# One more pair of chunks transposed on TensorE, and one load issued earlier, in a fused retention and MLP kernel

## The chip, the cores and the metric

The kernel runs on one NeuronCore of a Trainium2 chip. The metric is the device time of one execution in microseconds (us), lower is better. Every comparison of times is made between executions on the same chip.

## The reference, cut to what matters

The operation is a retention layer (attention without softmax, with a decay mask) followed by a two-layer MLP with the Mish activation. All inputs and the output are fp32.

```python
# q, k, v: [8 batches, 8 heads, 576 positions, 64]
scores = scale * np.matmul(q, k.transpose(0, 1, 3, 2))          # scale = 1/8
gamma  = 1.0 - 2.0 ** (-5.0 - np.arange(H))                     # one decay per head
Dmat   = np.where(rel >= 0, gamma[:, None, None] ** rel, 0.0)   # rel = i - j, causal
attn   = np.matmul(scores * Dmat, v)
x      = attn.transpose(0, 2, 1, 3).reshape(8 * 576, 512)       # 4608 tokens
h      = x @ w_in                                               # 512 -> 2048
g      = h * np.tanh(np.log1p(np.exp(h)))                       # Mish
out    = g @ w_out                                              # 2048 -> 512
```

## The kernel before: the parts that matter here

The 4608 tokens are 36 chunks of 128 tokens. Two chunks, `2m` and `2m + 1`, make a **pair** `m` (0 to 17), and four chunks make a **tile of tokens** `t` (0 to 8), the unit of the MLP. The kernel is one hand-ordered program: matmuls of the MLP, which fill TensorE (PE), are interleaved with the smaller steps of the retention, which prepare the tokens that the MLP needs next. The order on each engine is the order of the code.

The life of a pair `m`, from load to x:

- `load(m)`: GpSimd (POOL) issues three DMAs, q, k and v of both chunks. They go into buffers that rotate (4 for q and k), so `load(m)` waits until `step_p(m - 4)` has read the old contents.
- `step_p(m)`: VectorE (DVE) multiplies q and k by the decay factors into `qks`, in bf16, tokens on partitions. Four instructions to a pair.
- `step_t(n)`: q and k have to be turned, so that the head dimension lies on partitions (`qkT`). There are two ways. For chunks below `NPE`, PE transposes eight 128x128 blocks to a chunk (against an identity matrix) into PSUM, and then ScalarE (ACT) copies q's half and DVE k's half into `qkT`. From `NPE` on, one DMA, issued by SyncE (SP), transposes all 16 blocks of the pair from SBUF to SBUF.
- `step_s(n)`: PE computes the scores, DVE applies the mask (`sm`).
- `pair_o(m)`: PE adds up the state (`step_k`), then the products within the chunk and across chunks; DVE casts the sum into `xT`, the MLP's input.

```python
    NPE = 14
    # ...
    def step_t(n):
        m, u = divmod(n, 2)
        r = pairs[m]
        if "qk" not in r:
            r["qk"] = tr.tile([P, 2, 2, NP, P], BF16, name="qkT", bufs=3)
        if n >= NPE:
            nc.sync.dma_start_transpose(out=r["qk"].rearrange("p i u n t -> p (i u n) t"),
                                          in_=r["qks"].rearrange("p i u h d -> p (i u h d)"))
            return
        tp = ps_sc.tile([P, 4, NP, P], BF16, name="sc")[:, ::2]
        for i in range(2):
            flat = r["qks"][:, i, u].rearrange("p h d -> p (h d)")
            for p in range(NP):
                nc.tensor.transpose(tp[:, i, p, :], flat[:, ts(p, P)], ident)
        for i, copy in enumerate((nc.scalar.copy, nc.vector.tensor_copy)):
            copy(r["qk"][:, i, u], tp[:, i])
```

The part of the schedule that the change touches. `g1(t, i)` is the i-th of 16 steps of the MLP's first product (four matmuls of 512 columns, then Mish on ACT), `g2(t, i)` a quarter of a 128-token output tile (four matmuls); `one(n, "T")` and `one(n, "S")` call `step_t(n)` and `step_s(n)`. `cross(m)` is the transposing DMA, and it has a tail: GpSimd copies one element of the result, so that nothing which GpSimd issues later, above all the next `load`, starts before the transpose has landed.

```python
    def visit(m, w):
        n = 2 * m
        if w == 0:
            if 2 * m + 2 < NPE:
                load(m + 4)
        elif w == 2:
            if m == 5:
                step_sum(*step_k(1))
            if n < NPE:
                one(n, "T")
        elif w == 3 and n < NPE:
            one(n + 1, "T")
        elif w == 5:
            one(n, "S")
            one(n + 1, "S")
        elif w == 6 and m == 6:
            step_p(7)
        elif w == 7 and m < 6:
            pair_o(m, lambda: step_p(m + 1))

    def cross(m):
        step_t(2 * m)
        nc.gpsimd.tensor_copy(seen, pairs[m]["qk"][0:1, 0, 0, 0, 0:1])
    # ...
    for i in range(nF):                     # nF = 16
        visit(6 + i // 8, i % 8)            # pairs 6 and 7
        if i == 8:
            cross(7)
            load(10)
            step_p(8)
        elif i == 10:
            cross(8)
            load(11)
        g1(2, i)
        if i % 8 == 7:
            pair_o(6 + i // 8)
            if i == 15:
                scores(8)                   # step_s(16), step_s(17)
            for j in range(4):
                g2(1, 8 + i // 2 - 3 + j)

    for t in range(3, nT + 1):              # the steady loop
        for i in range(nF):
            m, w = 2 * (t + 1) + i // 8, i % 8
            if m + 1 < n_pairs and w == 0:
                step_p(m + 1)
            elif m + 1 < n_pairs and w == 2:
                cross(m + 1)
                load(m + 4)
            if t < nT:
                g1(t, i)
            if i % 4 == 3:
                if m < n_pairs and w == 7:
                    pair_o(m)
                    if m + 1 < n_pairs:
                        scores(m + 1)
                for j in range(4):
                    if t < nT or i < 12:
                        g2(t - 1, i - 3 + j)
```

So with `NPE = 14` pairs 0 to 6 are turned by PE and pairs 7 to 17 by DMA, and `load(10)` and `load(11)` each stand behind a transposing DMA.

Of the kernel before, what the change touches and what calls it, by code (L numbers as in the profile page):

```python
# [17 lines left out]
def kernel(  # L18
# [30 lines left out]
    nF = d_ff // P  # L49
    KC = d_model // P  # L50
    NCH = 4
    NPE = 14


    chunks = []
# [41 lines left out]
    def load(m):  # L97
        if m >= n_pairs:
            return
        r = pairs[m] = {}  # L100
        r["q"] = io.tile([P, 2, H, D], F32, name="qraw")
        r["k"] = io.tile([P, 2, H, D], F32, name="kraw")
        if m < NCH // 2:
            r["v"] = io.tile([P, 2, H, D], F32, name="vraw", bufs=NCH // 2)
            return
        r["vs"] = tok.tile([P, 2, H, D], BF16, name="v", bufs=5)
        if m < NCH:
            return
        for x, src in (("q", q), ("k", k), ("vs", v)):
            off = 0  # L110
            for b, i0, ni in chunks[2 * m]:
                nc.gpsimd.dma_start(  # L112
                    out=r[x][ds(off, ni)].rearrange("p u h d -> p (u h) d"),
                    in_=src[ds(b, 2), :, ds(i0, ni), :].rearrange("b h p d -> p (b h) d"))
                off += ni
# [139 lines left out]
    def step_p(m, us=(0, 1)):  # L255

        r = pairs[m]
        if "qks" not in r:
            r["qks"] = io.tile([P, 2, 2, H, D], BF16, name="qks")
            r["ks"] = r["qks"][:, 1]  # L260
        for u in us:
            for i, (x, g) in enumerate((("q", gq), ("k", gk))):
                nc.vector.tensor_tensor(  # L263
                    by_slots(r["qks"][:, i, u]), r[x][:, u].rearrange("p (r s) d -> p r s d", r=2),
                    g[:, place(2 * m), :].rearrange("p (r s) -> p r s", r=2).unsqueeze(3).to_broadcast([P, 2, NP, D]),
                    op=OP.mult)
# [18 lines that stand above are left out]
# [39 lines left out]
    def step_k(m):  # L324

        if m >= n_pairs or len(chunks[2 * m]) > 1:
            return None
        b, i0, _ = chunks[2 * m][0]
        ks, vs = pairs[m]["ks"], pairs[m]["vs"]

        if m < 6:
            st = ps_sc.tile([P, 2, 2, NP, 64], F32, name="sc")[:, 0]
        else:
            st = ps_h.tile([P, 2, NP, 64], F32, name="hp")
        for u in range(2):
            for p in range(NP):
                for e in range(2):
                    nc.tensor.matmul(st[ds(64 * e, 64), u, p, :], lhsT=ks[:, u, 2 * p + e, :],  # L338
                                     rhs=vs[:, u, 4 * e + p, :],
                                     start=(u == 0 and p == 0), stop=True, skip_group_check=True)  # L340
        return b, i0, st

    def step_sum(b, i0, st):

        if i0 == 0:
            st_sum[b] = tr.tile([P, 2, NP, 64], F32, name="st")
            nc.vector.tensor_copy(st_sum[b], st)
        else:
            nc.vector.tensor_tensor(st_sum[b], st_sum[b], st, op=OP.add)  # L349
        ssb = tr.tile([P, 2, NP, 64], BF16, name="ssb", bufs=6)  # L350
        (nc.vector.tensor_copy if b < 4 and i0 < 2 * P else nc.scalar.copy)(ssb, st_sum[b])  # L351
        for u in range(2):
            st_sb[b + u, i0 + P] = ssb[:, u]
# [41 lines left out]
    def pair_o(m, then=None):  # L395

        sc = pairs[m][1][0]
        ot = sc.rearrange("p e (g u) i -> p e g u i", g=2)
        state = step_k(m)
        for u in range(2):  # L400
            within(pairs[m]["vs"][:, u], pairs[m][u][1], ot[:, :, :, u, :], u == 0)
        for u in range(2):
            across(2 * m + u, ot[:, :, :, u, :])
        xt, s = x_of(2 * m)
        xv = xt[:, :, ds(s * P, 2 * P)].rearrange("p (e g) (u i) -> p e g u i", e=2, u=2)
        if m == 5:

            nc.scalar.copy(xv[:, 0], ot[:, 0])
            nc.vector.tensor_copy(xv[:, 1], ot[:, 1])
        else:  # L410
            nc.vector.tensor_copy(xv.rearrange("p e g u i -> p (e g) u i"), ot.rearrange("p e g u i -> p (e g) u i"))  # L411
        if then:
            then()
        if state:
            step_sum(*state)
# [5 lines left out]
    def g1(t, f):  # L421
        if f == 0:
            gts[t] = gp.tile([P, nF, NCH * P], BF16, name="gT")
        hp = ps_h.tile([P, NCH * P], F32, name="hp")
        for c in range(KC):
            nc.tensor.matmul(hp, lhsT=w_in_t[:, c, ts(f, P)], rhs=xts[t][:, c, :],  # L426
                             start=(c == 0), stop=(c == KC - 1))
        nc.scalar.activation(gts[t][:, f, :], hp, AX.Mish)  # L428
# [24 lines left out]
    def g2(t, i):  # L453
        s, part = divmod(i, 4)
        if t == nT - 1:
            s = (s + 2) % 4
        if part == 0:
            outs[t] = ps_h.tile([P, d_model], F32, name="hp")
        ops = outs[t]
        for f in range(4 * part, 4 * part + 4):  # L460
            nc.tensor.matmul(ops, lhsT=gts[t][:, f, ts(s, P)], rhs=w_out_t[:, f, :],  # L461
                             start=(f == 0), stop=(f == nF - 1))
        if part == 3:
            store(t, s, ops, nc.scalar.copy)
# [24 lines left out]
    def one(n, steps):  # L489
        for step in steps:  # L490
            if step == "P":
                step_p(n // 2, (n % 2,))
            else:
                {"T": step_t, "S": step_s, "O": step_o}[step](n)
# [96 lines left out]
# [6 lines that stand above are left out]
        elif w == 2:  # L597
            if m == 5:
                step_sum(*step_k(1))
            if n < NPE:  # L600
                one(n, "T")
        elif w == 3 and n < NPE:
            one(n + 1, "T")
        elif w == 5:
            one(n, "S")
# [11 lines that stand above are left out]
    def scores(m):  # L617
        one(2 * m, "S")
        one(2 * m + 1, "S")
# [3 lines left out]
    for i in range(nF):  # L623
        if i == 4:
            step_p(4)
        elif i >= 8:
            visit(4, i % 8)
        g2(0, i)
    for i in range(8):
        visit(5, i)  # L630
        g2(1, i)
    for i in range(nF):
        visit(6 + i // 8, i % 8)
        if i == 8:
            cross(7)
            load(10)
            step_p(8)
        elif i == 10:
            cross(8)
# [5 lines that stand above are left out]
                scores(8)  # L645
            for j in range(4):
                g2(1, 8 + i // 2 - 3 + j)

    for t in range(3, nT + 1):
        for i in range(nF):  # L650
            m, w = 2 * (t + 1) + i // 8, i % 8
# [46 lines left out]
```

## Time and profile before

| | |
|---|---|
| device time, three executions | 316.04, 316.23 and 316.77 us, median 316.23 |
| span of the profiled execution (316.77 us) | 315.0 us |
| PE busy | 299.9 us, 95% of the span |
| ACT, DVE, POOL busy | 134.8, 121.3, 79.2 us |
| DMA | 43.90 MB, mean 139 GB/s |
| transposing DMAs of `qks` into `qkT` | 11, issue to landing 4.2 us at least, 4.3 median, 10.4 at most |

How to read the profile's lines: times are us from the start of the span unless marked ns. PE is the matmul stream and PEld the weight loads beside it; SPq is the queue of SyncE, which issues DMAs. `L282` is line 282 of the kernel: L282 is the transpose on PE, L284 its copies to SBUF, L275 the transposing DMA, L112 the loads, L615 the one-element copy of `cross`, L308 the scores, L426 the MLP's first product, L461 its second, L484 the output's stores. `out<-in` names the tiles, and what stands in square brackets is the engine's idle time before the instruction and what ended it. The chain of waits is the sequence of work that ended last, followed backwards from the end.

### The profile page before, as it was taken

The numbers are of one execution on the slowest core, as the hardware profiler recorded it, in microseconds if no ns is written. First come the engines' busy times: TensorE is split into PE (matmuls) and PEld (weight loads), VectorE is DVE, ScalarE is ACT, GpSimd is POOL, SyncE is SP. The second block draws the span as 40 slices with busy tenths as digits, with TensorE's granted clock in tenths as the row PEclk, the third lists the DMA queues.
The fourth block names the chain that finished last, engine by engine and source line by source line (L and its number), as shares of the span: only waits on it lengthen the run. The fifth ranks groups of instructions, "written<-read, shape, count | busy, mean of one in ns | idle before, by whom it ended". The sixth has DMA issues, their size and how long they took to land.

```text
span 315.0 us, 6021 instructions
## 1 busy us (share of the span) xinstructions
PE 299.9 (95%) x2585; PEld 157.0 (50%) x2621; DVE 121.3 (38%) x170; ACT 134.8 (43%) x236; POOL 79.2 (25%) x103
## 2 busy tenths in 40 slices
PE   7799999999999898999999999999999999999995
PEld 3355588655554444444445454545454544444444
DVE  3456474218687471608080807070717141000000
ACT  7565656420464343344444434343434343334311
POOL 6676772543300620422404040500000000000000
PEclk9799999999999999999999999999999999999999
DMA  5999999999982999699797969793132300000032
GB/s 150 264 182 229 199 207 223 203 227 255 205 140 54 190 204 178 144 167 197 161 146 152 152 126 178 155 160 85 53 82 56 80 33 35 33 33 33 35 83 83
DMA packets 74026, 43.90 MB, mean 139 GB/s; under 512 B 57744, under 2 KB 65168, under 8 KB 74000
## 3 DMA queue, kind: packets, MB, share of 16 engines
q0 software_dynamic: 43424, 26.22, 56.4%
q1 hardware_dynamic: 30432, 17.18, 22.1%
q8 instruction: 20, 0.33, 0.5%
q10 hardware_dynamic: 144, 0.13, 0.1%
q14 instruction: 6, 0.05, 0.0%
HBM read 36.70 MB, written 9.44 MB: 146 GB/s over the span
## 4 chain that ended last, share of the span: by engine, by line
PE 83%; DMA 6%; ACT 4%; issue 2%; DVE 2%; SPq 1%; ACTq 0%; DVEq 0%
PE hp L461 37%; PE hp L426 29%; DMA qkT<-qks 5%; PE hp L449 4%; PE sc L308 3%; PE sc L360 3%; ACT res L481 2%; PE sc L374 1%; SPq L142 1%; DMA kraw<-in_k_dram 1%; PE hp L338 1%; PE hp L473 1%; PE sc L282 1%; PE hp L437 1%; ACT qkT L284 1%
## 5 line engine op out<-in xcount | busy, mean ns | idle before, releaser
L461 PE MATMUL hp<-w_out_t,gT 128*128 128x512 bf16 x541 | 125.2, 379 | 1.2 <-issue 0.3
L426 PE MATMUL hp<-xT,w_in_t 128*128 128x512 bf16 x480 | 112.6, 379 | 1.0
L428 ACT ACTIVATE gT<-hp 128x512 bf16<-128x512 f32 x124 | 74.0, 597 | 37.8 <-PE hp L426 35.2
L461 PEld LDWEIGHTS <-gT 128*128 128x128 bf16 x560 | 53.3, 98 | 62.7
L426 PEld LDWEIGHTS <-w_in_t 128*128 128x128 bf16 x496 | 47.7, 97 | 57.1 <-issue 0.3
L481 ACT COPY res<-hp 128x512 f32<-128x512 f32 x35 | 20.5, 586 | 81.4 <-PE hp L461 81.4
L411 DVE CAST xT<-sc 128x1024 bf16<-128x1024 f32 x13 | 15.9, 1224 | 97.3 <-PE sc L374 78.3
L318 DVE TENSOR_TENSOR sm<-sc,mask 128x1024 bf16<-128x1024 f32 x34 | 40.3, 1219 | 11.5 <-PE sc L308 11.5
L615 POOL COPY seen<-qkT 1x1 bf16<-1x1 bf16 x11 | 1.9, 177 | 130.8 <-DMA qkT<-qks 130.8
L263 DVE TENSOR_TENSOR qks<-kraw,gk 128x512 bf16<-128x512 f32 x32 | 21.9, 685 | 1.7 <-DMA kraw<-in_k_dram 1.7
L351 ACT CAST ssb<-st 128x512 bf16<-128x512 f32 x12 | 7.4, 618 | 34.5 <-DVE st L349 30.4
L263 DVE TENSOR_TENSOR qks<-qraw,gq 128x512 bf16<-128x512 f32 x32 | 21.9, 684 | 0.7 <-DMA qraw<-in_q_dram 0.7
L112 POOL DMA_DIRECT2D qraw<-in_q_dram x16 | 17.4, 1087 | 8.7 <-issue 3.5
L112 POOL DMA_DIRECT2D kraw<-in_k_dram x16 | 17.2, 1076 | 8.6 <-issue 4.1
L112 POOL DMA_DIRECT2D v<-in_v_dram x16 | 17.3, 1081 | 7.2 <-DMA kraw<-in_k_dram 2.5
L476 DVE COPY half<-hp 128x256 f32<-128x256 f32 x1 | 0.4, 424 | 43.8 <-PE hp L473 43.8
L449 PE MATMUL hp<-xT,w_in_t 128*128 128x128 bf16 x272 | 16.9, 219 | 0.2 <-ACT gT L451 0.2
L308 PE MATMUL sc<-qkT 64*128 64x128 bf16 x288 | 12.2, 220 | 4.4 <-DMA qkT<-qks 3.0
L449 PEld LDWEIGHTS <-w_in_t 128*128 128x128 bf16 x272 | 15.5, 98 | 0.9 <-issue 0.4
L308 PEld LDWEIGHTS <-qkT 64*128 64x128 bf16 x288 | 8.2, 95 | 10.3 <-DMA qkT<-qks 3.6
L451 ACT ACTIVATE gT<-hp 128x512 bf16<-128x512 f32 x17 | 10.0, 596 | 6.7 <-PE hp L449 6.7
L360 PE MATMUL sc<-sm,v 128*64 128x128 bf16 x288 | 12.2, 223 | 0.5 <-DVE sm L314 0.2
(70 smaller groups left out, 154.2 us busy)
## 6 DMA issues: line engine op xcount, KB each, us to landing
out_dram<-res SPq DMA_DIRECT2D x31, 256.0 KB, 2.1
qraw<-in_q_dram POOLq DMA_DIRECT2D x12, 512.0 KB, 8.2
kraw<-in_k_dram POOLq DMA_DIRECT2D x12, 512.0 KB, 9.7
v<-in_v_dram POOLq DMA_DIRECT2D x12, 256.0 KB, 10.6
qraw<-in_q_dram POOLq DMA_DIRECT2D x8, 256.0 KB, 9.7
kraw<-in_k_dram POOLq DMA_DIRECT2D x8, 256.0 KB, 9.4
w_out_t<-in_moe_w_out_dram POOLq DMA_DIRECT2D x4, 512.0 KB, 11.4
qraw<-in_q_dram SPq DMA_DIRECT2D x8, 128.0 KB, 3.3
```

The source lines that it names most:

```text
L112: nc.gpsimd.dma_start(out=r[x][ds(off, ni)].rearrange("p u h d -> p (u h) d"), in_=src[ds(b, 2), :, ds(i0, ni), :].rearrange("b h p d -> p ...
L263: nc.vector.tensor_tensor(by_slots(r["qks"][:, i, u]), r[x][:, u].rearrange("p (r s) d -> p r s d", r=2), g[:, place(2 * m), :].rearrange( ...
L308: nc.tensor.matmul(sc[:, e, p, :], lhsT=qk[r, 1, u, p, :], rhs=qk[r, 0, u, p, :], start=True, stop=True)
L318: nc.vector.tensor_tensor(sm.rearrange("p e n i -> p (e n) i"), sc.rearrange("p e n i -> p (e n) i"), mask1.rearrange("p e n i -> p (e n) ...
L360: nc.tensor.matmul(ot[ds(64 * c, 64), e, g, :], lhsT=vs[:, h, :], rhs=sm[:, e, p, :], start=(start and g == 0), stop=True, skip_group_chec ...
L411: nc.vector.tensor_copy(xv.rearrange("p e g u i -> p (e g) u i"), ot.rearrange("p e g u i -> p (e g) u i"))
L426: nc.tensor.matmul(hp, lhsT=w_in_t[:, c, ts(f, P)], rhs=xts[t][:, c, :], start=(c == 0), stop=(c == KC - 1))
L428: nc.scalar.activation(gts[t][:, f, :], hp, AX.Mish)
L449: nc.tensor.matmul(hp[:, j, :], lhsT=w_in_t[:, c, ts(4 * fb + j, P)], rhs=xts[t][:, c, ts(s, P)], start=(c == 0), stop=(c == KC - 1))
L451: nc.scalar.activation(gts[t][:, ds(4 * fb, 4), ts(s, P)], hp, AX.Mish)
L461: nc.tensor.matmul(ops, lhsT=gts[t][:, f, ts(s, P)], rhs=w_out_t[:, f, :], start=(f == 0), stop=(f == nF - 1))
L481: copy(ot, ops)
```

## The change

`NPE` goes from 14 to 16, so that pair 7 (chunks 14 and 15) is turned by PE and ACT/DVE copies, as pairs 4 to 6 are, and no longer by a DMA. Its two `step_t` calls then fall in `visit(7, 2)` and `visit(7, 3)`, two and three steps of `g1` after the place where the DMA was called. With `cross(7)` its one-element copy on GpSimd goes. The load of pair 10 moves as well: `visit(6, 0)` now issues it (`2 * 6 + 2 < 16`), eight steps of `g1` earlier, with no transposing DMA ahead of it. `load(11)` stays behind `cross(8)`.

The purpose is to take away a wait of PE for the DMA transpose of pair 7 where PE has plenty of matmuls to place around it, and to spread the loads of pairs 10 and 11.

```diff
-    NPE = 14
+    NPE = 16
@@ visit
         elif w == 2:
             if m == 5:
                 step_sum(*step_k(1))
-            if n < NPE:
-                one(n, "T")
-        elif w == 3 and n < NPE:
+            one(n, "T")
+        elif w == 3:
             one(n + 1, "T")
@@ first products of tile 2, second half of tile 1's second product
     for i in range(nF):
         visit(6 + i // 8, i % 8)
         if i == 8:
-            cross(7)
-            load(10)
             step_p(8)
         elif i == 10:
             cross(8)
```

In the order of instructions PE gains 16 transposes of 128x128 (eight ahead of step 10 of `g1(2, ...)` and eight ahead of step 11), ACT and DVE two copies of 128x512 each; SP loses one transposing DMA and GpSimd one copy. Nothing else moves.

## The prediction

> **What bounds the kernel now.** I read the first two parts of the page, then the chain of waits, then PE's timeline and windows around the changed place, and last the queues that PE waits for there. The page first: PE's total, PE by slice of 7.9 us, and the DMA's share by slice.
>
> ```profile
> PE 299.9 (95%) x2585; PEld 157.0 (50%) x2621; DVE 121.3 (38%) x170; ACT 134.8 (43%) x236; POOL 79.2 (25%) x103
> ...
> PE   7799999999999898999999999999999999999995
> ...
> DMA  5999999999982999699797969793132300000032
> ```
>
> PE is the bound from start to end. After the first two slices, which are start-up and not touched, only the 14th and the 16th slice (102 to 110 us and 118 to 126 us) fall to 8. In the 12th and 13th slice (87 to 102 us) the DMA share drops to 8 and 2 tenths: the DMA engines have nothing to do just ahead of the first dip. The chain of waits names both dips; here each stands between the pieces around it (start, length, what).
>
> ```profile
> 88.92 0.45 PE sc L282 x8
> ...
> 99.07 1.13 PE hp L426 x6
> 100.20 4.59 DMA qkT<-qks
> 104.79 0.05 issue
> 104.83 0.62 PE sc L308 x16
> ...
> 113.43 2.50 PE hp L426 x12
> 115.93 10.40 DMA qkT<-qks
> 126.33 0.05 issue
> 126.38 0.62 PE sc L308 x16
> ```
>
> These are the only two places where the end hangs on a transposing DMA: pair 7's, issued at 100.20 and landed after 4.59 us, and pair 9's, issued at 115.93, which took 10.40 us. PE has other work during most of both. What it really loses is the bracket in its timeline, the idle time ahead of the scores:
>
> ```profile
> 104.83 0.62 PE L308 MATMUL sc<-qkT 64*128 64x128 bf16 x16 [1.43 <-DMA qkT<-qks]
> ...
> 126.38 0.62 PE L308 MATMUL sc<-qkT 64*128 64x128 bf16 x16 [1.61 <-DMA qkT<-qks]
> ```
>
> The same view with all other scores shows no such bracket after these two: from 132 us on the windows give PE 15.58 us busy in each 15.70. So 1.43 + 1.61 = 3.04 us are at stake, 1.0% of the span, and no more. Why the second DMA took 10.40 us stands in the timelines of SP and POOL:
>
> ```profile
> 77.87 1.16 POOL L112 DMA_DIRECT2D qraw<-in_q_dram  x1 [2.67 <-DVE qks L263]
> ...
> 104.84 0.18 POOL L615 COPY seen<-qkT 1x1 bf16<-1x1 bf16 x1 [23.06 <-DMA qkT<-qks]
> 105.52 1.15 POOL L112 DMA_DIRECT2D qraw<-in_q_dram  x1 [0.50 <-issue]
> ...
> 111.35 1.17 POOL L112 DMA_DIRECT2D v<-in_v_dram  x1
> ```
>
> POOL finishes issuing load 9 at 81.8, then stands 23.06 us behind pair 7's transpose, and then issues loads 10 and 11 together from 105.5 to 112.5. The transpose of pair 9 goes out into that backlog. In the list of windows, 96 to 100 us has a DMA share of 0.00, and 112 to 120 us one of 1.66 and 1.22.
>
> **What the Trainium skill says.** "VectorE: DVE Perf Modes", section "The three transpose paths", puts a 128x128 bf16 transpose at 390 ns on TensorE and 1309 ns by DMA. "TensorE: Matmul & The Clock Gate", section "Part 4: PE-mode transpose", adds about 275 ns in a kernel, and that PSUM has to be copied out. The trace has 219 ns for one, and eight in 0.45 us on the chain (56 ns each), since they are pipelined; the measured 0.45 is what I use. The DMA moves 16 blocks in 4.59 us, 287 ns each, far less than the page's single block. "DMA: Bandwidth & Descriptors", section "Issuing engines are not separate DMA queues", says that DMAs run on the same 16 engines and interleave, whoever issues them. The trace agrees: landing times of the transpose go from 4.2 us on idle engines to 10.40 beside the two loads. The same page, section "Queues, rings and completion order", has each engine take turns between queues by packets, so a transpose is slowed, not held until a load is done.
>
> **The change part by part.**
>
> *Removed: pair 7's DMA and the wait for it.* PE no longer waits for it at 103.41. That is -1.43 us.
>
> *Added on PE: 16 transposes* in two groups of eight, each between steps of `g1`. Two rows of the chain show a group between such steps, at 87.61 and 88.92 us, 0.45 us each, with PE going on at once. So +0.90 us. The scores' own 0.55 us and everything else stay.
>
> *Are these scores ready in time?* PE reaches step 10 of this stretch at 98.91 plus two steps of 0.865 (20 matmuls in 4.33 us), with the chain's boundary some 0.15 later: about 100.8. The first group ends near 101.2, the second near 102.6. The input is there, since DVE multiplied pair 7 by 96.2. ACT needs 0.58 us to a copy and DVE 0.42, one after the other: the second group is in SBUF at about 103.2 to 103.8, with room for a Mish of 0.60 ahead of it. The scores start at about 103.41 + 0.90 = 104.3. So no wait, with 0.5 us in hand, just what pair 6 has (its copy ends at 90.48, its scores start at 91.02). On ACT there are 0.60 + 0.58 = 1.18 us of work to a step of 0.865 + 0.45 = 1.31, so the Mish steps keep up; the two PSUM banks of `g1` don't stall PE, as they don't at 88 us.
>
> *Moved: load 10.* Its q buffer is free when DVE has read pair 6's q, at 87.9. POOL then issues q, k, v in three steps of 1.15 us, to about 91.4. Load 9 drains until about 91.5. Load 10 has 1.31 MB (512 + 512 + 256 KB); at the 215 GB/s that the DMA listing shows for a load alone this takes 6.1 us. So it lands at about 98, in the stretch where the engines stood still, ahead of the store at 99.76 and of pair 8's transpose.
>
> *Pair 8's transpose* goes out when DVE has finished pair 8 (100.37), lands at about 105, and is needed at 108.8. No wait.
>
> *Load 11* is released by it at about 105.5, now alone: 1.31 MB done by about 112.7 rather than behind load 10.
>
> *Pair 9's transpose* is issued at 115.93 - 0.52 = 115.4, as its inputs follow PE. The path to its scores moves as well, so they would start at 124.77 - 0.52 = 124.25 if nothing held them: 8.85 us after the issue, as before. With load 11 done, the engines carry only an output store, so the landing should be the 4.3 us median, at about 120. The wait goes: -1.61 us.
>
> *Sum:* -1.43 + 0.90 - 1.61 = -2.14 us. On the profiled execution that is 316.77 - 2.14 = 314.6; on the median 316.23 - 2.14 = 314.1. The saved time reaches the end, because PE has no slack behind 126 us that could take it up. The two waits depend on DMA timing, and the profiled execution was the longest of three, by 0.54 us over the median, so its waits may have been longer than usual. I take a little off the saving and set 314.3 us.
>
> **The rivals.**
>
> *Only the first wait goes.* If pair 9's transpose is slow for another reason than the two loads (the store before it, or being long by nature), the second wait stays, and the gain is 1.43 - 0.90 = 0.5 us: 315.7. For it: the transpose of pair 10, issued at 131.77 with a single load ahead of it, needed 7.7 us. Against it: later ones with no load in flight land in 4.2 to 4.3 us, and even 7.7 is below the 8.85 allowed. I give it 15%.
>
> *A new wait in the place of the first.* If ACT's copies fall behind the Mish steps, the scores of chunk 15 wait for `qkT`. For it: ACT is then at 1.18 of 1.31 us, DVE starts its copy only after ACT's, and the margin is 0.5 us. Against it: pairs 5 and 6 went through the same sequence with DVE much busier. It would cost 0.3 to 0.6 us: about 314.7. I give it 15%.
>
> *The earlier load disturbs its surroundings.* POOL issues it from 87.9 to 91.4, while DVE works on pair 6's state and copies with 0.5 us of margin before its scores at 91.02. For load 9, at 77.87 to 81.8, DVE did the same kinds of work at the usual durations (0.68, 0.43, 0.45 us), so I expect nothing. If it did disturb: up to 0.5 us.
>
> *The transposes cost more than the waits.* At 219 ns each without overlap 16 of them would be 3.5 us and eat the gain: 317. The rows with 0.45 us for eight speak against it, 3%.
>
> **Range and chances.** The best case is both waits gone and the executions like the median, about 314.0, with 0.5 us below that for spread; the case of one wait kept is 315.7. The first is much more likely, so the range for 8 in 10 is 313.5 to 315.6. A gain of over 2% would need 309.9 us, more than all waits of PE on these DMAs; a loss of over 2% would need 322.6. Faster 1%, within 2% 98%, slower 1%.
>
> **What the profile afterwards would show.** Right: PE's timeline has two groups of x8 L282 near 101 and 102 us and no bracket ahead of L308 near 104; the DMA share of 92 to 98 us is no longer near zero; the transpose of pair 9 lands in less than 8.8 us and L308 near 124 follows L374 without a bracket; ten transposing DMAs remain. Wrong: a bracket ahead of L308 near 104 that names ACT or DVE; a bracket near 124 that still names the DMA; a wait of DVE for pair 8's or 9's inputs; or new idle time of PE later, which would show that the end hangs on something other than PE's own stream.

## The result, and the profile after

| | before | changed |
|---|---|---|
| device time, median of four executions | 316.26 us (316.04 to 316.77) | 314.07 us (313.58 to 314.68) |
| span of the profiled execution | 315.0 us | 311.9 us |
| transposing DMAs, issue to landing (shortest, median, longest) | 4.2, 4.3, 10.4 us | 4.2, 4.3, 4.3 us |

The ratio of the times is 0.9929, with a 95% interval of 0.9905 to 0.9954: 2.2 us less.

The page of the changed kernel, its busy times and the slices of PE and DMA:

```profile
PE 300.8 (96%) x2601; PEld 157.7 (51%) x2637; DVE 122.8 (39%) x172; ACT 135.9 (44%) x238; POOL 78.4 (25%) x102
...
PE   7889999999999999999999999999999999999995
...
DMA  5999999999999696959696969792323201000132
```

Both dips of PE are gone, and the hole in the DMA's 12th and 13th slice has filled from 8 and 2 tenths to 9 and 6: load 10 moves there now. Two parts of the chain of waits show what PE does in place of waiting (start, length, what):

```profile
98.21 1.74 PE hp L426 x8
99.95 0.45 PE sc L282 x8
100.40 0.86 PE hp L426 x4
101.26 0.45 PE sc L282 x8
101.71 1.51 PE hp L426 x7
103.22 0.15 issue
103.37 0.62 PE sc L308 x16
...
122.35 0.57 PE sc L360 x16
122.92 0.38 PE sc L374 x32
123.29 0.55 PE sc L308 x16
```

The two groups of eight transposes cost 0.45 us each, and the scores of pair 7 follow the matmuls (one of the 20 L426 records is missing, hence the 0.15). At 123.29 the scores of pair 9 follow L374 directly. No transposing DMA is left in the chain in this part. L360 and L374 are the products within and across chunks, which end pair 8's `pair_o`. (L614 is the L615 of before: the changed file is a line shorter there.) POOL's timeline shows the moved load and its consequence:

```profile
87.52 1.15 POOL L112 DMA_DIRECT2D qraw<-in_q_dram  x1 [5.69 <-DVE qks L263]
...
103.96 0.18 POOL L614 COPY seen<-qkT 1x1 bf16<-1x1 bf16 x1 [13.00 <-DMA qkT<-qks]
104.58 1.16 POOL L112 DMA_DIRECT2D qraw<-in_q_dram  x1 [0.44 <-issue]
...
118.84 0.18 POOL L614 COPY seen<-qkT 1x1 bf16<-1x1 bf16 x1 [10.80 <-DMA qkT<-qks]
```

Load 10 goes out at 87.5 to 91.0, held only by DVE's reading of the old contents. Load 11 goes out alone at 104.58. Pair 9's transpose, issued at 114.45, has landed when POOL copies its element at 118.84.

Where the 3.1 us between the two profiled spans come from can be read off three marks on PE. The first step of `g1(2, ...)` starts at 99.07 before and at 98.21 after: 0.86 us that arose in the start-up, where the two kernels are the same (see the end). From there to pair 7's scores it takes 5.76 us before and 5.16 after: 0.60 less. From there to pair 9's scores it takes 21.55 and 19.86: 1.69 less. The end of the second stretch is the start that PE's timeline gives; the chain puts it at 123.29, because a piece of the chain begins where the piece before it ends.

```profile
123.23 0.62 PE L308 MATMUL sc<-qkT 64*128 64x128 bf16 x16
```

The rest is the same: every later group of scores is 3.15 or 3.16 us earlier than before. So the change is worth 2.2 us, and it is best read as a stretch that begins after the start-up. Below, "the stretch" is the span less the start of pair 6's L338 on PE (the products that add up the state, `step_k`): 315.0 - 94.27 = 220.7 us before, 311.9 - 93.41 = 218.5 after.

### The profile page after: what moved, and what is told of

It is laid out like the page before. It is cut to its first block, busy times and chain, and to the rows that moved or that the text cites. A ratio compares the mean times of both kernels' runs of the same rounds, so it can differ in the third digit from the quotient of the medians.

```text
span 311.9 us, 6052 instructions
## 1 busy us (share of the span) xinstructions
PE 300.8 (96%) x2601; PEld 157.7 (51%) x2637; DVE 122.8 (39%) x172; ACT 135.9 (44%) x238; POOL 78.4 (25%) x102
## 4 chain that ended last, share of the span: by engine, by line
PE 87%; ACT 4%; DMA 3%; SPq 2%; issue 2%; DVE 1%; POOL 0%; ACTq 0%; POOLq 0%
PE hp L461 39%; PE hp L426 32%; PE hp L449 4%; PE sc L308 3%; PE sc L360 3%; SPq L142 2%; ACT res L481 2%; DMA w_in_t<-in_moe_w_in_dram 2%; PE sc L374 2%; DMA kraw<-in_k_dram 1%; PE sc L282 1%; PE hp L338 1%; PE hp L473 1%; ACT qkT L284 1%; PE sc L338 1%
## 5 line engine op out<-in xcount | busy, mean ns | idle before, releaser
L426 PE MATMUL hp<-xT,w_in_t 128*128 128x512 bf16 x480 | 112.8, 379 | 1.0
L426 PEld LDWEIGHTS <-w_in_t 128*128 128x128 bf16 x496 | 47.6, 98 | 56.6 <-issue 0.3
L614 POOL COPY seen<-qkT 1x1 bf16<-1x1 bf16 x10 | 1.8, 177 | 122.1 <-DMA qkT<-qks 122.1
L449 PE MATMUL hp<-xT,w_in_t 128*128 128x128 bf16 x272 | 16.9, 219 | 0.2 <-ACT gT L451 0.2
L449 PEld LDWEIGHTS <-w_in_t 128*128 128x128 bf16 x272 | 15.5, 98 | 0.9 <-issue 0.4
L284 DVE COPY qkT<-sc 128x512 bf16<-128x512 bf16 x12 | 5.1, 423 | 20.0 <-ACT qkT L284 19.9
L360 PE MATMUL sc<-sm,v 128*64 128x128 bf16 x288 | 12.0, 221 | 0.6 <-DVE sm L314 0.4
```

The lines of the kernel that those rows point to most:

```text
L360: nc.tensor.matmul(ot[ds(64 * c, 64), e, g, :], lhsT=vs[:, h, :], rhs=sm[:, e, p, :], start=(start and g == 0), stop=True, skip_group_chec ...
L449: nc.tensor.matmul(hp[:, j, :], lhsT=w_in_t[:, c, ts(4 * fb + j, P)], rhs=xts[t][:, c, ts(s, P)], start=(c == 0), stop=(c == KC - 1))
```

## The experiments

My theory has two parts: the DMA transpose of pair 7 is exchanged for cheaper work on PE, and the second wait was made by loads 10 and 11 going out together. The main rival says that taking a DMA out of SP's queue did it all; others are with the experiments. The first four share one set of runs of the kernel before on the same chip (median 316.43 us), the last two another (316.00 us).

| run | median us | ratio to before, 95% interval | stretch, us |
|---|---|---|---|
| kernel before | 316.43 and 316.00 | 1 | 220.7 |
| changed kernel, again | 314.25 | 0.9938 (0.9917 to 0.9959) | 218.5 |
| loads 10 and 11 together | 315.34 | 0.9959 (0.9942 to 0.9977) | 219.6 |
| only the load early | 314.79 | 0.9938 (0.9912 to 0.9965) | 219.1 |
| DMA early, load early | 313.23 | 0.9910 (0.9886 to 0.9935) | 217.6 |
| transposes three times | 315.99 | 0.9991 (0.9975 to 1.0007) | 220.3 |
| only the DMA early | 313.74 | 0.9926 (0.9903 to 0.9950) | 218.0 |

The intervals are some 0.5% wide, as wide as what is asked; so the verdicts rest on the stretches and on the waits in the traces, and the medians support them. Each stretch is that of one profiled execution, and the profiles are not all from one chip.

### The changed kernel again

No edit. 

> The changed kernel once more, with more rounds, beside the experiments on one chip. Both theories expect what was measured: 2.0 to 2.3 us less than before, with no idle time of PE ahead of the scores of pair 7 and of pair 9.

Measured: a ratio of 0.9938, and a stretch of 218.5 us as in the first profile. PE has no wait on a DMA in the changed part. The stretch of this kernel repeats to 0.1 us, while the span of the two profiles differs by 0.8.

### Both loads together again

```diff
 # against the changed kernel
-            if 2 * m + 2 < NPE:
+            if 2 * m + 2 < NPE - 2:
                 load(m + 4)
@@
             cross(8)
+            load(10)
             load(11)
```

> Pair 7 on PE as in the changed kernel, but loads 10 and 11 both held behind pair 8's transpose, so that they go out together at about 104 us again. My theory (the second wait came from the backlog of the two loads): pair 9's transpose takes about 10 us again, PE waits 1.2 to 1.8 us for it, and only 1.43 - 0.90 = 0.5 us of the gain is left, about 315.7. Rival (taking pair 7's DMA out of SP's queue is enough, the loads don't matter): no second wait, about 314.1.

Measured: 315.34 us and a stretch of 219.6, so half of the gain is gone: 1.1 us are left, where I had expected 0.5. The timelines of PE and SP, and what the list of `qkT`'s instructions gives as landing times of the transposing DMAs (shortest, median, longest):

```profile
124.90 0.62 PE L308 MATMUL sc<-qkT 64*128 64x128 bf16 x16 [1.05 <-DMA qkT<-qks]
```

```profile
115.02 6.28 SPq L275 DMA_TRANSPOSE qkT<-qks  x1
```

```profile
DMA to landing us min/median/max: 4.2/4.3/9.8
```

With pair 7 on PE, and only the loads bunched again, pair 9's transpose takes 9.8 us in place of 4.3, and the bracket ahead of its scores is back. The rival falls: the second wait belongs to the loads. The wait is 1.05 us, a little below the 1.2 that I had as the lower end, as the transpose was 0.6 us quicker than before's 10.40. Why it was quicker is not shown.

### Only the load early

```diff
 # against the kernel before
-            if 2 * m + 2 < NPE:
+            if 2 * m + 2 < NPE + 2:
                 load(m + 4)
@@
             cross(7)
-            load(10)
             step_p(8)
```

> Pair 7 by DMA as before, and only the load of pair 10 moved ahead of it. My theory: the first wait of about 1.4 us stays, the second goes, so 1.6 us less than before, about 314.6. Rival (the loads don't matter): as before, 316.2.

Measured: 314.79 us and a stretch of 219.1, which is 1.6 less than before. PE's timeline at the three scores:

```profile
104.68 0.62 PE L308 MATMUL sc<-qkT 64*128 64x128 bf16 x16 [1.41 <-DMA qkT<-qks]
...
109.10 0.62 PE L308 MATMUL sc<-qkT 64*128 64x128 bf16 x16
...
124.54 0.62 PE L308 MATMUL sc<-qkT 64*128 64x128 bf16 x16
```

The first wait stays as it was (1.41), the second is gone. So the moved load alone is worth 1.6 of the 2.2 us, and on top of it the work moved to PE only the 0.6 left over. The two don't simply add up: with the loads together the work on PE gave 1.1 us alone, because the second wait was shorter there as well (1.05 us for 1.61).

### The DMA one step earlier, and the load early

Before, pair 7's inputs are ready at 96.2 us, but its transpose is issued at 100.20, because SP issues in order and an output store stands ahead of it, which waits for its data until 99.76 (ACT's copy of them ends at 99.74). These are DVE's last product for pair 7 and SP's timeline in the kernel before; the x2 counts pair 8's transpose too:

```profile
95.54 0.69 DVE L263 TENSOR_TENSOR qks<-kraw,gk 128x512 bf16<-128x512 f32 x1
```

```profile
99.76 0.33 SPq L484 DMA_DIRECT2D out_dram<-res  x1
100.20 4.91 SPq L275 DMA_TRANSPOSE qkT<-qks  x2
```

Here the call moves one step up, ahead of that store.

```diff
 # against the kernel with only the load early
-        if i == 8:
+        if i == 7:
             cross(7)
+        elif i == 8:
             step_p(8)
```

> Pair 7 by DMA, but issued one step earlier, ahead of an output store in SP's queue that held it up from 96.2 to 100.2 us; load of pair 10 early. My theory: the transpose lands near 101, ahead of its scores at 103.4, the second wait is gone as well, and PE has no transposes to do: 3.0 us less than before, about 313.2, 0.9 us better than the changed kernel. Rival (the DMA transpose is too slow there wherever it is issued, and the work has to be on PE): a wait of about 1 us stays, 314.2 or more.

Measured: 313.23 us and a stretch of 217.6, 3.1 less than before and 0.9 less than the changed kernel. The timelines of SP and PE:

```profile
97.48 2.90 SPq L275 DMA_TRANSPOSE qkT<-qks  x1
100.95 0.35 SPq L484 DMA_DIRECT2D out_dram<-res  x1
101.61 2.23 SPq L275 DMA_TRANSPOSE qkT<-qks  x1
```

```profile
104.52 0.62 PE L308 MATMUL sc<-qkT 64*128 64x128 bf16 x16
...
108.94 0.62 PE L308 MATMUL sc<-qkT 64*128 64x128 bf16 x16
...
124.38 0.62 PE L308 MATMUL sc<-qkT 64*128 64x128 bf16 x16
```

(This execution's start-up was 2 us longer than that of the changed kernel's profile; pair 6's L338 starts at 95.46.) The transpose now goes ahead of the store, and none of the three scores has a bracket. This version gets rid of both waits, as the changed kernel does, and saves PE the 0.9 us of transposes. It has the lowest time and the shortest stretch of all that ran; by the medians alone its interval still overlaps that of the changed kernel.

### The transposes three times over

```diff
 # against the changed kernel
-            for p in range(NP):
-                nc.tensor.transpose(tp[:, i, p, :], flat[:, ts(p, P)], ident)
+            for p in range(NP * (3 if n in (14, 15) else 1)):
+                nc.tensor.transpose(tp[:, i, p % NP, :], flat[:, ts(p % NP, P)], ident)
```

> The changed kernel with each of pair 7's 16 transposes done three times over into the same place, so 32 more on PE and nothing else. My theory (eight in 0.45 us, the cost is PE's own time): 1.8 us more than the changed kernel, about 316.0, and still no wait at either scores. Rival (a transpose costs PE its full 219 ns, the sum only came out by luck): 7.0 us more, about 321. If part of the groups hid behind waits, less than 0.9 us more.

Measured: 315.99 us and a stretch of 220.3, 1.8 above the changed kernel. The chain of waits:

```profile
101.03 1.34 PE sc L282 x24
...
103.07 1.50 PE sc L282 x24
```

24 transposes in 1.34 us are 56 ns each (the second 1.50 holds a missing matmul record ahead of it). Each added transpose costs PE its 56 ns in full, nothing of it hides and nothing comes on top, and no wait appears. So 0.90 us for 16 is their price.

### Only the DMA early

```diff
 # against the kernel before
-        if i == 8:
+        if i == 7:
             cross(7)
             load(10)
+        elif i == 8:
             step_p(8)
```

> Pair 7 by DMA, issued one step earlier, with the load of pair 10 still behind it. My theory: the first wait goes (1.43 us). Load 10 now goes out at about 101.5, just as pair 8's transpose starts, and slows it to 6 to 8 us, landing at 107 to 108.5, with its scores due at 107.4: a new wait of 0 to 1 us. Load 11 follows it at about 108, so that pair 9's transpose at 114.5 meets a smaller backlog than before: no second wait, or one below 0.5 us. In all 1.5 to 3.0 us less than before, 313.2 to 314.7. Rival (only the early load of pair 10 cures the second wait): 1.4 us less, about 314.9.

Measured: 313.74 us and a stretch of 218.0, 2.7 less than before. The chain of waits at the new place, and PE's timeline:

```profile
100.30 7.65 DMA qkT<-qks
```

```profile
108.00 0.62 PE L308 MATMUL sc<-qkT 64*128 64x128 bf16 x16 [0.30 <-DMA qkT<-qks]
...
123.44 0.62 PE L308 MATMUL sc<-qkT 64*128 64x128 bf16 x16
```

Load 10, issued from 101.24, meets pair 8's transpose and makes it 7.65 us long; its scores, which never waited before, wait 0.30 us. Pair 9's transpose is issued at 114.30 and POOL sees it at 122.82, some 8.5 us later: slowed again, but in time. From its issue to 117 us the DMA listing has only the loads' queue moving, so load 11 is what it met. The rival (only the early load cures the second wait) falls: it is enough that load 10 goes out 4 us earlier. What counts is that the transpose lands while PE has other work, some 9 us from its issue (8.8 in the changed kernel, 9.1 here): 8.4 us were short enough, 9.8 and 10.40 were not.

## Why the prediction was right, point by point

- *The bound and what is at stake.* PE's two brackets, 1.43 + 1.61 us, were said to be all there is. The version without either wait and without added work on PE came out 3.1 us shorter in its stretch, against 3.04. Right. Each wait cost a little more than its bracket: from pair 6's L338 to pair 7's scores it takes 10.56 us before and 9.06 with the early DMA, 1.50 for a bracket of 1.43.
- *Removed and added at pair 7.* Predicted -1.43 + 0.90 = -0.53 us, measured -0.60 between the two marks, which is the 1.50 less 0.90. The 0.90 is confirmed by doing the transposes three times over.
- *Scores of pair 7 in time.* Predicted for 104.3, with the last copy done by 103.8. In the changed kernel DVE's last copy ends at 102.82, the scores start at 103.37, 0.55 us later: the margin of 0.5 us was right. The rival of a wait for ACT and DVE did not come.
- *Load 10.* Predicted to go out at 87.9 and to be done by about 98. It went out at 87.52; the DMA listing has 0.48 MB of POOL's queue moved from 94 to 97 us, 0.07 MB from 97 to 98.5 and 0.01 MB in the next microsecond, so it ended at about 98.8, ahead of pair 8's transpose at 99.56. The order was right, the size was not: this execution was through its start-up 0.86 us sooner, so that the forecast for its end was 97.1. The load took 1.7 us longer, since its last 0.07 MB moved at 47 GB/s in place of the 215 that the sum had used. Load 11 too ended later than forecast (113.8 us, for 111.8), 0.65 ahead of pair 9's transpose.
- *The rival that load 10 disturbs its surroundings.* DVE's cast ahead of its copies lasts 0.61 or 0.62 us in all five profiles that issue load 10 early, and 0.43 in the other three, so something was disturbed; what slows it is not shown. It cost nothing: the last copy for pair 6 ends 0.54 us ahead of the scores in both kernels.
- *Pair 9's transpose.* Predicted to land after 4.3 us and the wait of 1.61 to vanish. It landed after 4.3, and the mark-to-mark time fell by 1.69. How the loads hold it up is not quite as predicted ("slowed, not held"). In the kernel before, the DMA listing of 114 to 119 us has 1.05 MB in the loads' queue and nothing in the queue of stores and transposes, although a store had been issued at 114.12 and the transpose at 115.93. The turns between queues, on which the prediction relied, show only from 119 us on, when 0.26 MB of the loads were left. So the transpose stood still first and shared the engines then. The rival that it would stay slow had its ground in pair 10's 7.7 us; that one ran beside load 12, which now goes out 7.6 us earlier (119.48 for 127.09), and it takes 4.3 us as well.
- *The sum.* Predicted -2.14 us, measured 2.2 in both the stretch and the medians; 314.3 was set, 314.07 and 314.25 were measured. The little that I took off, for waits that might be longer than usual in the profiled execution, can't be checked with one trace of the kernel before; the sum didn't need it.

What the prediction did not ask was why pair 7's transpose was late in the first place. It read the issue at 100.20 and the 4.59 us from there, but not the 4 us ahead of it. SP's order was the cause, and the change pays 0.9 us on PE for what a call one step of `g1` earlier gives for nothing.

## What to carry to other kernels

A wait on a DMA has two ends: when it was issued and what was in flight beside it. Look at both before moving its work to the busiest engine; here moving one load and one call did more than moving the work. When a load is gated by something unrelated, as load 10 was by a transpose, check what it collides with when it comes loose. And ask of every transfer in an in-order queue what the instruction ahead of it waits for.

## What the runs showed that I had not expected

In all eight profiles PE runs the same instructions up to pair 6, and yet its L338 starts anywhere from 93.41 to 95.46 us. That is up to 2.1 us between executions, as much as the gain under study, and all of it arises in the first 40 us: from a group of 32 matmuls (L449) that starts between 38.74 and 40.79 us, every one of the eight takes 54.67 or 54.68 us to L338. A first guess is the granted clock. The windows of 8 to 16 us of the second and the first profile of the changed kernel (columns: start and end, length, busy time of PE, PEld, DVE, ACT and POOL, clock, DMA share, GB/s):

```profile
8.00:16.00 8.00, 6.00 (x47) 2.68 (x45) 3.88 (x8) 4.41 (x8) 4.88 (x8) 0.79 1.05 262
```

```profile
8.00:16.00 8.00, 6.45 (x70) 3.34 (x67) 4.97 (x9) 5.29 (x10) 5.45 (x9) 1.00 1.10 272
```

With 0.79 the mark is at 94.19, with 1.00 at 93.41. But over all eight it doesn't hold: the four profiles with 0.79 there have marks at 93.97, 94.19, 94.27 and 95.46, the four with 1.00 at 93.41, 94.14, 94.15 and 94.49. So the clock doesn't decide the order, and the cause stays open; it was not tried. What helps is to measure from a mark behind the start-up: the two profiles of the changed kernel agree to 0.1 us there.
